# Gated mix of a diagonal state-space layer and a long convolution: another work plan, C loaded in halves, angle tables in integers, filler matmuls at the start

## The chip, the cores and the metric

The kernel runs on one core of a Trainium2 chip. A core has five engines that run side by side and meet at semaphores: TensorE (PE, matrix products into PSUM), VectorE (DVE), ScalarE (ACT), GpSimd (POOL) and SyncE (SP, which here only issues transfers). The metric is the device time of one execution in microseconds (us). The three timed executions of the kernel before took 474.46, 478.96 and 480.90 us; their median, 478.96 us, is what the changed kernel is measured against. One more execution was profiled: it took 469.38 us, of which 467.6 us lie between its first and its last instruction. Every duration below is from that execution.

## The reference, cut to what matters

`x` is 2048 by 1024 (time by channel), bfloat16; P = 1024 states.

```python
g = sigmoid((x * gate_w).sum(-1))                     # one gate per time step
# a: diagonal complex state space
Lam_bar = exp(dt * Lam);  B_bar = ((Lam_bar - 1) / Lam)[:, None] * Bmat
Bu = einsum("bld,pd->blp", x, B_bar)
for t in range(L):  h = Lam_bar * h + Bu[:, t];  hs.append(h)
a = 2 * einsum("blp,dp->bld", hs, Cmat).real + x * Dskip
# b: short convolution of k (4 taps), times v, long convolution over time, times x
kv = shift_conv(k, shift_k) * v
y  = irfft(rfft(pad(kv)) * rfft(pad(ssm_k)))[:S] + kv * ssm_D
b  = x * y
return g * a + (1 - g) * b
```

## The kernel before, in words

Three families of work share the engines.

**State space (`s5`).** The 1024 states are 8 blocks of 128 (`pi`). For a block: `loadB` loads B's rows, `prep` builds six scaled identities (`dg`) and from them B-bar transposed (`BT`, two PSUM groups), `gemm_u` multiplies BT with x transposed (`xT`, eight tiles, loaded by transposing DMAs from SP) for odd and even times and two chunks `c` of 512, `tables` makes sine and cosine rows, `rot` turns the recurrence into a real scan on DVE, `odd` rebuilds the odd steps. The states `Hc` go out to a scratch `h_scr` in DRAM and come back as `Hr`, except for the last NKEEP blocks, which stay (`Hk`).

**Convolution (`conv`).** The 1024 channels are 8 units of 128. `kvprep` makes kv (transposing loads from SP, taps on DVE, or on ACT by the planner's choice) and writes it to `kv_scr`. The long convolution is a discrete Fourier transform in two levels: `stage1` (8 PSUM groups in a unit), `spec` (8, with the tables fC, fS, fN), `product` on DVE, `inverse` (4, with gC, gS, gN), copies by DMA into `zb`, and `final` (2), which writes x times y into `pB_scr`. Where a unit's two `final` groups stand says how far the convolution is.

**Output (`outp`).** Sixteen tiles: two halves `dh` of 512 channels, and in each of them eight groups of 256 times. A tile needs all states, C transposed (`CT`), and `pb`: the rows of `pB_scr` of four convolution units, scaled by ACT (`sc`) and DVE (`pre`). The half dh = 0 needs units 0 to 3, dh = 1 units 4 to 7. A tile is two runs of 16 matmuls, each 128x128 by 512 columns.

Every PSUM group is emptied by `evac`, an ACT copy that the planner may give to DVE. PSUM has four buffers.

**What sets the order.** Each piece is an `op` with an engine, an assumed duration and a priority. `_Plan.schedule` plays them through a list scheduler, which also places tiles in 21 slabs of SBUF and the four PSUM buffers; the result is a fixed instruction order for each engine. A tile tagged `hold` (CT, Hr) is placed only if `fits_after` finds room left for the others. A table of constants (S0, C1, CT0 and so on) sets the priorities. On the chip each engine runs its list strictly in order, waiting at semaphores, whatever the assumed durations were. Both kernels build this list before the launch, so the list can be read without any time in it.

In the lists of before, PE's first output matmul comes when all 64 `stage1` groups, all 64 `spec` groups, 30 of 32 `inverse` groups and 12 of 16 `final` groups are behind it; after the last `final` group 336 output matmuls are left. ACT runs 216 evac copies, DVE 26. POOL issues ten loads of `Hr`, 512 KB each, in one row.

Of the kernel before, what the change touches and what calls it, by code (L numbers as in the profile page):

```python
# [34 lines left out]
class _Plan:  # L35
# [5 lines left out]
    def __init__(self, nslab, nps):  # L41
        self.ops = []
        self.tags = {}
        self.nslab, self.nps = nslab, nps
        self.nbig, self.horizon = 4, 40.0
        self.late = ("xn", "pb", "ot", "Hk")
# [63 lines left out]
    def schedule(self, free0):  # L110
# [35 lines left out]
        def fits_after(t):  # L146
# [166 lines left out]
def kernel(  # L313
# [65 lines left out]
    nc.vector.memset(pihalf_col, math.pi / 2.0)  # L379
    ident = consts.tile([128, 128], BF16, name="ident")  # L380
# [4 lines left out]
    nc.scalar.activation(out=dummy, in_=pihalf_col, func=ACT.Exp)  # L385
    nc.tensor.matmul(psums[0][:, 0:24], lhsT=prow, rhs=ident[0:24, 0:24], start=True, stop=True)
# [118 lines left out]
    def evac(o_, i_, r, w, prio):  # L505
        op("ACT", 1.03, lambda: A.copy(o_(), i_()), r=r, w=w, prio=prio, alt=("DVE", 1.2, lambda: V.tensor_copy(o_(), i_())))  # L506
# [11 lines left out]
    XE = -536.86  # L518
    NSPL = 2
    GP0 = -233.73  # L520
    GP1 = -1426.02
    GP2 = 37.38
    BNCAP = 6
    PUNTIL = 45.26
    ZBCAP = 4
    NKEEP = 3
    HCAP = 5
    TABCAP = 3
    ZCAP = 10
    KVCAP = 2  # L530
    QQCAP = 2
    RACAP = 5
    RBCAP = 8
    KTCAP = 1
    ABCAP = 7
    PPCAP = 2
    TMCAP = 3
    OTCAP = 3
    BTCAP = 9
    S0 = 36.23  # L540
    S1 = 1.67
    C0 = 37.21
    C1 = 2.59
    CB = 0.59
    CT0 = 102.49
    CT1 = 6.46
    HR0 = 24.45
    HRc = 2.62
    KP0 = -5.46
    KP1 = -0.7  # L550
    KPu = 6.73
    KA0 = -11.86
    VA0 = -49.96
    FN0 = 6.99
    TB0 = -218.72
    TB1 = 6.46
    XS0 = -59.09
    PN0 = 7.58
    RT0 = 10.11
    OD0 = 20.44  # L560
    UE0 = 11.29
    D10 = -11.04
    GPR = (GP0, GP1, GP2)
    QB, QA = "POOL", "SP"
    CTP = lambda i: CT0 + CT1 * i
# [14 lines left out]
    def tables0():  # L580
# [53 lines left out]
        mF = pl.tile("tgZ", [16, 128], F32, cap=3)  # L634
        qF = pl.tile("tgZ", [16, 128], F32, cap=3)

        def f1():
            V.tensor_copy(mF.ap, mi.ap)
# [494 lines left out]
```

## Time and profile before

| what | value |
|---|---|
| median of the runs (lowest, highest) | 478.96 us (474.46, 480.90) |
| profiled execution, and its span | 469.38 us, 467.6 us |
| PE busy | 423.5 us, 2722 matmuls |
| DVE busy | 345.6 us |
| ACT busy | 306.7 us |
| POOL busy | 50.0 us |
| moved by DMA | 74.18 MB |
| first output matmul starts at | 334.22 us |
| last `final` matmuls end at | 390.4 us |
| last matmul ends at | 462.8 us |

How to read it: "busy" is the time in which an engine had an instruction running. Matmuls are pipelined: one of 512 columns is listed with some 380 ns, but in a dense row one starts every 216 ns, so that a gap of up to 0.16 us between two matmuls does not show as idle time. The table of windows has a row for each stretch of time: its length, then the busy time of PE, PE's weight loads, DVE, ACT and POOL with the number of instructions, the clock granted to PE as a share of full speed, the mean busy share of the DMA engines and the GB/s that they moved. A row of a timeline has its start, its duration, engine, line and operation; behind it, in brackets, how long the engine had been idle and what it waited for. In the kernel of before, L506 is the evac copy, L1074 the output matmul, L870 `gemm_u`, L716 `stage1`, L729 to L731 `spec`, L756 to L758 `inverse`, L775 and L776 `final`, L832 `prep`, L976 the gate's matmul, L499 and L501 the issue of a transposing and of a plain DMA.

### The profile page before, as it was taken

How to read it: one execution, taken by the hardware profiler on the slowest of the kernel's cores; microseconds unless marked ns; L12 is line 12 of the kernel's file. 1: busy time of each engine (PE TensorE's matmuls, PEld its weight loads, DVE VectorE, ACT ScalarE, POOL GpSimd, SP SyncE). 2: the span in 40 equal slices, each digit the busy share in tenths (PEclk: the TensorE clock that was granted, in tenths of full speed). 3: DMA queues.
4: the chain of work that ended last, by engine and by line, in shares of the span. 5: the costliest groups of instructions: out<-in, count | busy, mean ns of one | idle time of the engine just before them, and what ended most of it. 6: DMA issues, size and time to landing. Idle time of an engine off the chain costs nothing.

```text
span 467.6 us, 7311 instructions
## 1 busy us (share of the span) xinstructions
PE 423.5 (91%) x2722; PEld 232.3 (50%) x2722; DVE 345.6 (74%) x606; ACT 306.7 (66%) x342; POOL 50.0 (11%) x61
## 2 busy tenths in 40 slices
PE   2989699997988989999999999998769899999996
PEld 0434456664644655564665655665424444444442
DVE  5997989978988898898897998799613626445432
ACT  3579998969998996799799988679301332212210
POOL 9656010100100100100000000040000000000000
PEclk9999999998999998999999999999959999999999
DMA  8999391987799896595589373399999976243221
GB/s 192 167 163 243 73 254 61 237 169 136 168 225 184 197 203 136 184 202 127 147 148 181 88 161 89 80 171 318 192 199 177 218 179 178 71 134 96 86 67 45
DMA packets 169463, 74.18 MB, mean 159 GB/s; under 512 B 136066, under 2 KB 164754, under 8 KB 169428
## 3 DMA queue, kind: packets, MB, share of 16 engines
q1 hardware_dynamic: 164996, 58.75, 62.6%
q0 software_dynamic: 4368, 14.97, 10.4%
q8 instruction: 21, 0.34, 0.3%
q14 instruction: 14, 0.11, 0.1%
q10 hardware_dynamic: 64, 0.01, 0.0%
HBM read 30.70 MB, written 17.83 MB: 104 GB/s over the span
## 4 chain that ended last, share of the span: by engine, by line
PE 61%; ACT 14%; DVE 8%; DMA 7%; SPq 5%; issue 4%; ACTq 0%; DVEq 0%
PE ps L1074 20%; PE ps L870 17%; ACT slab L506 9%; PE ps L729 4%; SPq L501 3%; PE ps L716 3%; PE ps L942 2%; PE ps L880 2%; PE ps L832 2%; PE ps L731 2%; PE ps L730 2%; DVE slab L506 2%; DMA slab<-kv_scr 2%; ACT slab L701 2%; PE ps L756 2%
## 5 line engine op out<-in xcount | busy, mean ns | idle before, releaser
L506 ACT CAST slab<-ps 128x1024 bf16<-128x1024 f32 x216 | 204.4, 1040 | 73.7 <-DMA slab<-slab 22.9
L1074 PE MATMUL ps<-slab,slab 128*128 128x512 bf16 x480 | 111.1, 385 | 8.6 <-DMA slab<-in_A_C_im_dram 3.4
L870 PE MATMUL ps<-slab,slab 128*128 128x512 bf16 x504 | 116.6, 380 | 1.5 <-DVE slab L506 0.9
L1074 PEld LDWEIGHTS <-slab 128*128 128x128 bf16 x512 | 50.4, 99 | 72.4 <-issue 14.7
L870 PEld LDWEIGHTS <-slab 128*128 128x128 bf16 x512 | 48.4, 98 | 58.2 <-issue 6.3
L1080 DVE SCALAR_TENSOR_TENSOR slab<-ps,gcols,slab 128x512 bf16<-128x512 f32 x32 | 23.2, 748 | 56.5 <-PE ps L1074 52.7
L1057 ACT ACTIVATE slab<-slab,omgc 128x512 bf16<-128x512 bf16 x32 | 21.4, 720 | 52.2 <-DMA slab<-pB_scr 51.6
L729 PE MATMUL ps<-slab,fC 128*128 128x512 bf16 x128 | 48.5, 379 | 3.5 <-ACT slab L506 3.4
L701 ACT ACTIVATE slab<-slab,skc 128x1024 bf16<-128x1024 bf16 (+3 forms) x37 | 41.7, 1166 | 3.7 <-DMA slab<-slab 3.1
L716 PE MATMUL ps<-tab,slab 128*128 128x128 bf16 x512 | 36.3, 221 | 7.8 <-ACT slab L506 5.8
L506 DVE CAST slab<-ps 128x1024 bf16<-128x1024 f32 x24 | 29.1, 1221 | 16.8 <-PE ps L758 10.3
L716 PEld LDWEIGHTS <-slab 128*128 128x128 bf16 x512 | 31.6, 98 | 13.7 <-issue 8.1
L731 PE MATMUL ps<-slab,fN 128*128 128x256 bf16 x128 | 34.9, 273 | 0.0
L730 PE MATMUL ps<-slab,fS 128*128 128x256 bf16 x128 | 34.9, 272 | 0.0
L703 DVE TENSOR_TENSOR slab<-slab,slab 128x1024 bf16<-128x1024 bf16 (+3 forms) x47 | 32.2, 685 | 2.3 <-ACT slab L701 2.3
L756 PE MATMUL ps<-slab,gC 128*128 128x256 bf16 x128 | 30.6, 277 | 2.5 <-DVE slab L746 1.3
L746 DVE TENSOR_TENSOR slab<-slab 128x512 bf16<-128x512 bf16 x64 | 25.4, 420 | 6.2 <-DMA slab<-slab 3.4
L743 DVE TENSOR_TENSOR slab<-slab 128x1024 bf16<-128x1024 bf16 x32 | 22.0, 688 | 10.0 <-DMA pB_scr<-slab 10.0
L757 PE MATMUL ps<-slab,gN 128*128 128x128 bf16 x128 | 28.4, 222 | 0.0
L758 PE MATMUL ps<-slab,gS 128*128 128x128 bf16 x128 | 28.4, 222 | 0.0
L742 DVE TENSOR_TENSOR slab<-slab 128x1024 bf16<-128x1024 bf16 x32 | 22.0, 687 | 1.5 <-DMA slab<-slab 0.8
L501 POOL DMA_DIRECT2D h_scr<-slab x10 | 5.4, 544 | 164.4 <-ACT slab L506 156.8
(177 smaller groups left out, 554.5 us busy)
## 6 DMA issues: line engine op xcount, KB each, us to landing
slab<-in_A_x_dram SPq DMA_DIRECT2D x32, 256.0 KB
slab<-slab SPq DMA_DIRECT2D x128, 64.0 KB
h_scr<-slab POOLq DMA_DIRECT2D x10, 512.0 KB, 4.0
slab<-h_scr POOLq DMA_DIRECT2D x10, 512.0 KB, 14.6
slab<-in_B_ssm_k_dram SPq DMA_DIRECT2D x8, 512.0 KB
kv_scr<-slab SPq DMA_DIRECT2D x8, 512.0 KB
slab<-kv_scr SPq DMA_DIRECT2D x8, 512.0 KB
pB_scr<-slab SPq DMA_DIRECT2D x16, 256.0 KB
```

The costliest lines, as they stand in the source:

```text
L506: op("ACT", 1.03, lambda: A.copy(o_(), i_()), r=r, w=w, prio=prio, alt=("DVE", 1.2, lambda: V.tensor_copy(o_(), i_())))
L701: alt=("ACT", 1.05, lambda: A.activation(out=tmp.ap[:, 0:n], in_=kT.ap[:, src], func=ACT.Copy, scale=skc[:, u, j:j + 1])))
L703: op("DVE", 0.74, lambda: TT(out=acc.ap[:, lo:hi], in0=acc.ap[:, lo:hi], in1=tmp.ap[:, 0:n], op=ALU.add), r=[acc, tmp], w=[acc], prio=pr)
L716: PE_.matmul(ps.ap[:, i, :], lhsT=a.ap[:, 8 * q + i, :], rhs=t1v[:, hh * 128:(hh + 1) * 128], start=True, stop=True)
L729: PE_.matmul(ps.ap[:, i], lhsT=fC[:, k2, :], rhs=zz, start=True, stop=False)
L730: PE_.matmul(ps.ap[:, i, :, 0, :], lhsT=fS[:, k2, :], rhs=zz[:, :, 1, :], start=False, stop=False)
L731: PE_.matmul(ps.ap[:, i, :, 1, :], lhsT=fN[:, k2, :], rhs=zz[:, :, 0, :], start=False, stop=True)
L756: PE_.matmul(ps.ap[:, i], lhsT=gC[:, k2, :], rhs=pp.ap[:, i], start=True, stop=False)
L757: PE_.matmul(ps.ap[:, i, 0, :], lhsT=gN[:, k2, :], rhs=pp.ap[:, i, 1, :], start=False, stop=False)
L758: PE_.matmul(ps.ap[:, i, 1, :], lhsT=gS[:, k2, :], rhs=pp.ap[:, i, 0, :], start=False, stop=True)
L870: PE_.matmul(ps.ap[:, ri, :], lhsT=BT.ap[:, d, ri, :], rhs=xT[d].ap[:, par, c0:c0 + CW], start=(d == 0), stop=(par == 1 and d == ND - 1))
L1074: PE_.matmul(ps.ap[:, ti, :], lhsT=Hr[pi, a // 4].ap[:, par, ri, (a % 4) * 128:(a % 4 + 1) * 128], rhs=CT[pi].ap[:, ri, ds_], start=(i == ...
```

## The change: what it does

1. **Room rules.** `fits_after` asks for less room: `least` tiles of a tag (one if none is given) instead of its full cap, plus `spare`; three slabs instead of four are kept for the big tiles.
2. **C in halves.** A CT tile holds 512 channels instead of 1024: 16 pairs of transposing loads of 128x512 instead of 8 pairs of 128x1024, with priorities of their own for dh = 0 and dh = 1. NKEEP goes from 3 to 4, so that eight chunks of state, not ten, go out to DRAM and come back.
3. **Priorities and durations.** All constants of the table are new, as are several assumed durations.
4. **Integer angle tables.** In `tables0` the product of indices is kept as an integer and reduced with a bitwise AND; the copy to float, the rounding and the subtraction go. ACT's sine takes the integer with a scale and a bias.
5. **Filler matmuls.** 24 matmuls of 128x128 by 128 columns on the identity ahead of the first real one, and 20 more (`keep`) for each of the eight x tiles of the first gate pass: 184 in all, whose results nobody reads.
6. **The first `dg`** is made in two halves, of which `prep` needs only the first.

```diff
+    for _ in range(24):
+        nc.tensor.matmul(psums[2][:, 0:128], lhsT=ident, rhs=ident, start=True, stop=True)
...
-            need = 1
+            need = 0
             for tg, (cap, size, hold) in caps.items():
-                if size and not hold and (size < 8192 or not big) and not (t.tag == "CT" and tg in self.late):
-                    need += min(cap - live.get(tg, 0), left[tg]) * size // 2048
-            return free >= need
+                if size and not hold and (size < 8192 or not big):
+                    need += max(0, min(self.least.get(tg, 1), cap) - live.get(tg, 0)) * size // 2048 if left[tg] else 0
+            return free >= need + self.spare
...
-    NKEEP = 3
+    NKEEP = 4
...
-    C1 = 2.59
+    C1 = 2.56
...
-            V.tensor_copy(mF.ap, mi.ap)
-            TS(out=mF.ap, in0=mF.ap, scalar1=iota_col, scalar2=1.0 / 8192.0, op0=ALU.mult, op1=ALU.mult)
-            TS(out=qF.ap, in0=mF.ap, scalar1=MAGIC, scalar2=-MAGIC, op0=ALU.add, op1=ALU.add)
-            TT(out=mF.ap, in0=mF.ap, in1=qF.ap, op=ALU.subtract)
+            TS(out=mi.ap, in0=mi.ap, scalar1=iota_col, scalar2=None, op0=ALU.mult)
+            TS(out=mi.ap, in0=mi.ap, scalar1=8191, scalar2=None, op0=ALU.bitwise_and)
...
-            TS(out=sc, in0=sc, scalar1=1.0 / 8192.0, scalar2=None, op0=ALU.mult)
             TT(out=mG.ap, in0=iota_row[:, 0:128].unsqueeze(1).to_broadcast([128, 16, 128]),
                in1=sc.unsqueeze(2).to_broadcast([128, 16, 128]), op=ALU.mult)
-            TS(out=qG.ap, in0=mG.ap, scalar1=MAGIC, scalar2=-MAGIC, op0=ALU.add, op1=ALU.add)
-            TT(out=mG.ap, in0=mG.ap, in1=qG.ap, op=ALU.subtract)
+            TS(out=mG.ap, in0=mG.ap, scalar1=8191, scalar2=None, op0=ALU.bitwise_and)
...
+                if par == 1 and d < NWARM:
+                    def keep():
+                        for _ in range(20):
+                            PE_.matmul(wps.ap[:, 0:128], lhsT=ident, rhs=ident, start=True, stop=True)
+                    op("PE", 20 * MM(128), keep, w=[wps], prio=pr)
...
-        def load_CT(pi, pr):
-            t = pl.tile("CT", [2, D], cap=8, hold=True)
+        def load_CT(pi, dh, pr):
+            t = pl.tile("CT", [2, 512], cap=16, hold=True)
...
-            load_CT(pi, CTP(i))
+            load_CT(pi, 0, CTP(i, 0))
...
+        for i, pi in enumerate(korder):
+            load_CT(pi, 1, CTP(i, 1))
...
-                outp(dh, par, a2, prio(base + 6.9 * k + D10 * dh))
+                outp(dh, par, a2, prio(base) + (SC1 * 6.9 * k if dh == 0 else SC1 * 55.0 + D10 + 6.9 * (k - 8)))
```

The lists that the planner makes of this differ on every engine. Two places matter here.

On SP, the queue of transfers, the first loads of C stood in one row in the kernel of before. In the rows, `slab` is a piece of SBUF and the number after it names the slab.

```order
L501 DMA slab_191<-in_A_x_dram 128x2x512
L501 DMA slab_182<-slab_186 8x16x256 x4
L499 DMA_TRANSPOSE slab_190<-in_A_C_re_dram 128x1024
L499 DMA_TRANSPOSE slab_190<-in_A_C_im_dram 128x1024
L499 DMA_TRANSPOSE slab_200<-in_A_C_re_dram 128x1024
L499 DMA_TRANSPOSE slab_200<-in_A_C_im_dram 128x1024
L499 DMA_TRANSPOSE slab_189<-in_A_C_re_dram 128x1024
L499 DMA_TRANSPOSE slab_189<-in_A_C_im_dram 128x1024
```

In the changed kernel the first of them stand between the convolution's copies into `zb` (the rows with 8x16x256) and the last write of kv.

```order
L509 DMA slab_212<-slab_215 8x16x256 x4
L509 DMA slab_221<-in_A_x_dram 128x8x128
L507 DMA_TRANSPOSE slab_215<-in_A_C_re_dram 128x512
L507 DMA_TRANSPOSE slab_215<-in_A_C_im_dram 128x512
L509 DMA slab_212<-slab_221 8x16x256 x4
L509 DMA kv_scr<-slab_215 128x2048
L507 DMA_TRANSPOSE slab_220<-in_A_C_re_dram 128x512
L507 DMA_TRANSPOSE slab_220<-in_A_C_im_dram 128x512
L509 DMA slab_224<-in_A_x_dram 128x2x512
L509 DMA slab_212<-slab_221 8x16x256 x4
```

The sixteen loads of before follow the last write of kv in one block; of the changed kernel's 32, the first pair comes ahead of it, eight pairs are issued ahead of the first output matmul's turn in the plan, and eight after it.

On PE, the first output matmuls (L1074) followed the 30th of the 32 `inverse` groups (L757, L758) in the kernel of before.

```order
L757 LDWEIGHTS gN
L757 MATMUL ps_92<-slab_193,gN 128x128
L758 LDWEIGHTS gS
L758 MATMUL ps_92<-slab_193,gS 128x128
L1074 LDWEIGHTS slab_186
L1074 MATMUL ps_94<-slab_190,slab_186 128x512
```

In the changed kernel (output L1097, `odd` L954 and L956) the first output tile stands ahead of the last block's second `odd` group, and convolution groups follow between the tiles.

```order
L1097 LDWEIGHTS slab_218
L1097 MATMUL ps_99<-slab_223,slab_218 128x512
L954 LDWEIGHTS ident
L954 MATMUL ps_98<-slab_219,ident 128x512
L956 LDWEIGHTS slab_224
L956 MATMUL ps_98<-slab_219,slab_224 128x512
```

What moved behind the first output matmul: 8 `stage1` groups, 12 `spec` groups, 6 `inverse` groups, 2 `final` groups and one `odd` group. After the last `final` group 320 output matmuls are left (336 before). ACT now runs 218 evac copies (DVE 24), and 29 multiplications of `kvprep` (43 before); POOL issues six loads of `Hr` and SP two, eight instead of ten.

More of the change, by code (lines that the diff above doesn't have):

```diff
@@ L821, in mk, with part @@
                                                  in1=dco[:, pi, :].unsqueeze(2).to_broadcast([128, 6, 128]), op=ALU.mult)
-            op("DVE", 0.9, mk(V), r=[e_dco], w=[dg], prio=pr - 5, alt=("POOL", 1.5, mk(G), PUNTIL))
+            if pi == 0:
+                for k in range(2):
+                    def part(k=k):
+                        V.tensor_tensor(out=dg.ap[:, 3 * k:3 * k + 3, :], in0=ident.unsqueeze(1).to_broadcast([128, 3, 128]),
+                                        in1=dco[:, pi, 3 * k:3 * k + 3].unsqueeze(2).to_broadcast([128, 3, 128]), op=ALU.mult)
+                    op("DVE", 0.5, part, r=[e_dco], w=[(dg, k)], prio=pr - 5)
+            else:
+                op("DVE", 0.97, mk(V), r=[e_dco], w=[(dg, 0), (dg, 1)], prio=pr - 5, alt=("POOL", 1.5, mk(G), PUNTIL))
             BT = pl.tile("BT", [ND, 2, 128], cap=BTCAP)
```

182 lines of the change are left out of this document (98 added, 84 removed).

## The prediction

> **What bounds the kernel now.** I read the busy times first, then the table of windows, then the waits of PE, and last the timelines around the places where PE stands still.
>
> ```profile
> PE 423.5 (91%) x2722; PEld 232.3 (50%) x2722; DVE 345.6 (74%) x606; ACT 306.7 (66%) x342; POOL 50.0 (11%) x61
> ...
> 0.00:12.00 12.00, 3.80 (x11) 1.09 (x12) 6.64 (x40) 4.30 (x11) 11.22 (x19) 1.00 0.85 193
> 12.00:24.00 12.00, 12.00 (x59) 5.23 (x57) 11.16 (x18) 6.57 (x12) 8.29 (x5) 1.00 1.17 163
> 24.00:36.00 12.00, 10.59 (x49) 3.60 (x48) 11.49 (x9) 7.72 (x9) 7.21 (x3) 1.00 1.11 170
> 36.00:60.00 24.00, 20.16 (x139) 10.79 (x139) 21.54 (x38) 23.87 (x24) 7.45 (x7) 1.00 0.76 149
> 60.00:180.00 120.00, 107.14 (x807) 66.22 (x805) 102.84 (x180) 108.83 (x114) 7.32 (x14) 0.97 0.85 184
> 180.00:300.00 120.00, 118.73 (x845) 70.97 (x843) 105.81 (x187) 102.19 (x112) 3.25 (x6) 1.00 0.65 139
> 300.00:334.00 34.00, 30.65 (x275) 20.82 (x273) 30.75 (x55) 28.21 (x31) 4.73 (x9) 1.00 1.02 223
> 334.00:352.00 18.00, 11.32 (x34) 3.71 (x34) 5.09 (x11) 1.01 (x1) 0.53 (x1) 0.72 0.96 198
> 352.00:366.00 14.00, 12.18 (x57) 5.29 (x56) 4.08 (x7) 2.02 (x2) 0.00 (x0) 1.00 0.96 181
> 366.00:390.00 24.00, 24.00 (x127) 11.71 (x127) 13.90 (x20) 8.56 (x12) 0.00 (x0) 1.00 0.77 188
> 390.00:462.75 72.75, 72.75 (x338) 32.85 (x336) 30.85 (x46) 13.42 (x20) 0.00 (x0) 1.00 0.32 97
> 462.75:467.60 4.85, 0.19 (x1) 0.00 (x0) 1.41 (x2) 0.00 (x0) 0.00 (x0) 1.00 0.16 54
> ```
>
> PE is the fullest engine, but only at the end is it the only one. From 390 us it is never idle, with DVE and ACT far below it. From 36 to 180 us ACT works as long as PE or longer (108.83 us beside 107.14), and PE is idle for 3.84 + 12.86 us. From 180 to 300 us ACT has 0.86 of PE's time, and PE is idle for 1.27 us in 120. That pair of rows is what I lean on most: PE's gaps come and go with ACT's load. From 334 to 352 us nothing is full: a hole.
>
> ```profile
> PE ps L716 <- ACT slab L506: 5.8, 11, 1.9
> PE ps L386 <- DMA prow<-in_A_Lambda_im_dram: 4.3, 1, 4.3
> PE ps L775 <- ACT slab L506: 4.1, 3, 2.0
> PE ps L729 <- ACT slab L506: 3.4, 5, 1.7
> PE ps L1074 <- DMA slab<-in_A_C_im_dram: 3.4, 4, 1.2
> ...
> 337.91 0.38 PE L1074 MATMUL ps<-slab,slab 128*128 128x512 bf16 x1 [1.23 <-DMA slab<-in_A_C_im_dram]
> ...
> 345.49 5.47 PE L1074 MATMUL ps<-slab,slab 128*128 128x512 bf16 x17 [0.58 <-DMA slab<-in_A_C_im_dram]
> ```
>
> Columns: total, times, longest, in us. Behind the parameters (L386), PE mostly waits for the evac copy on ACT; the hole is the wait for C.
>
> How much of the span is work that cannot go? The pace of a dense row is in the chain of waits:
>
> ```profile
> 11.59 3.23 PE ps L832 x16
> ...
> 22.95 0.87 PE ps L832 x8
> ...
> 222.48 0.89 PE ps L716 x16
> ...
> 390.42 72.53 PE ps L1074 x336
> ```
>
> So a matmul takes 0.216 us with 512 columns, 0.109 with 256 and 0.0556 with 128. The code issues 1408, 512 and 768 of them: 304.0 + 55.7 + 42.7 = 402.4 us. The span has 65.2 us more: 10.3 us ahead of 11.59 (11.59 less the 1.3 us that three gate pairs need), 1.5 us because `prep`'s 16 matmuls ran at half pace (3.23 us against twice 0.87), 4.85 us behind the last matmul, and 48.5 us between. Of those 48.5, 10.3 belong to the hole from 334 to 366 us: 6.68 and 1.82 idle, and 5.47 us for 17 matmuls that need 3.67. Idle time of 1.41, 3.84, 12.86, 1.27 and 3.35 us makes 22.7, and 15.5 are gaps too short to show as idle.
>
> **The change part by part.** *Start.* The 184 fillers cost 24 and 160 times 0.0556, 1.3 and 8.9 us at full pace. The first 24 run ahead of the parameters, for which PE waited 4.3 us, so they cost nothing. Of the 160, in PE's list, 120 stand ahead of `prep`: 6.7 us, into some 5 us that were lost there anyway (PE is idle 8.2 us of the first 12, 4.3 of them for the parameters, and six gate matmuls at `prep`'s half pace lose 1.3). So `prep` starts 1.7 us later and runs 1.5 us shorter. The other 40 stand between the gate's matmuls of the fourth and fifth x tile, where PE was full (12.00 of 12 us): 2.2 us later. Together +2.4 us.
>
> ```profile
> 15.67 1.22 DVE L638 CAST slab<-slab 128x2048 f32<-128x2048 int32 x1
> 16.92 1.28 DVE L639 TENSOR_SCALAR slab<-slab,iota_col 128x2048 f32<-128x2048 f32 x1
> ...
> 19.51 2.66 DVE L641 TENSOR_TENSOR slab<-slab,slab 128x2048 f32<-128x2048 f32 x1
> ...
> 33.54 2.29 DVE L663 TENSOR_TENSOR slab<-slab,slab 128x2048 f32<-128x2048 f32 x1
> ...
> 22.20 1.91 ACT L645 ACTIVATE fS<-slab 128x2048 bf16<-128x2048 f32 x1 [3.52 <-DVE slab L641]
> ...
> 35.87 1.91 ACT L645 ACTIVATE gS<-slab 128x2048 bf16<-128x2048 f32 x1 [4.18 <-DVE slab L663]
> ```
>
> The integer tables drop L638, L641, L663 and a rounding pass apiece; in their place comes an AND over 2048 integers, twice. No row shows that AND. Its bounds are 1.22 us (the cast, one input) and 2.66 us (the slowest pass of this size, two inputs); I take 1.28, since it too reads one tensor and a constant. The f table then needs two passes instead of four, the g table two instead of three, and DVE gets about 6.2 us back. ACT waited 3.52 and 4.18 us for just these results, and from 36 to 60 us it is full while PE idles 3.84 us behind it. I count 2.4 us of that as gained and the start as even, between -3 and +4 us: if the AND were slow, nothing would hide it, for DVE is busy 22.65 of the 24 us from 12 to 36.
>
> By the Trainium skill, "TensorE: Matmul & The Clock Gate", section "What's actually happening", PE is released to full clock after some 3.4 us of sustained work, whatever its number of matmuls; the 3.23 us of the 16 slow `prep` matmuls agree. By that rule the first 24 fillers, some 2.6 us at half pace, are not enough, and the next would lengthen the start by about 0.4 us, an estimate from that page; the sum does not contain it.
>
> *Load on ACT and DVE.* ACT gets 14 of 43 `kvprep` multiplications less and two copies more.
>
> ```profile
> L506 ACT CAST slab<-ps 128x1024 bf16<-128x1024 f32 x216 | 204.4, 1040 | 73.7 <-DMA slab<-slab 22.9 <-PE ps L758 12.0 <-PE ps L870 9.4
> L701 ACT ACTIVATE slab<-slab,skc 128x1024 bf16<-128x1024 bf16 (+3 forms) x37 | 41.7, 1166 | 3.7 <-DMA slab<-slab 3.1
> L694 ACT ACTIVATE slab<-slab,skc 128x2048 bf16<-128x2048 bf16 x6 | 12.2, 2038 | 0.0
> L742 DVE TENSOR_TENSOR slab<-slab 128x1024 bf16<-128x1024 bf16 x32 | 22.0, 687 | 1.5 <-DMA slab<-slab 0.8
> L746 DVE TENSOR_TENSOR slab<-slab 128x512 bf16<-128x512 bf16 x64 | 25.4, 420 | 6.2 <-DMA slab<-slab 3.4
> ```
>
> Nine of the short and five of the long ones go: 9 x 1.17 + 5 x 2.04 - 2 x 1.04 = 18.6 us off ACT. DVE takes them over, at 0.69 us at most for a short one (L742 has two inputs) and twice that for a long one: up to 13 us.
>
> *Convolution behind the first output tiles.* Moved there: 8 `stage1`, 12 `spec`, 6 `inverse`, 2 `final` groups, 28 evacs, 29 us of ACT or DVE copies; on DVE six products of 2 x 0.69 + 2 x 0.42, two multiplications and the one `rot` chunk that `odd` waits for (without its scans 4 x 0.69 + 4 x 0.42), 19 us; on PE, by the paces above, 3.6 + 10.4 + 5.2 + 1.7 + 1.3 for the `odd` group = 22 us. Up to 334 us, by the windows, ACT was busy for 281.7 us and DVE for 290.2; PE's useful work there is 402.4 less the 512 output matmuls (110.6) and the six groups that came later (5.2): 286.6 us. Now ACT has 281.7 - 18.6 - 24 (its share of the 29) = 239 us beside 286.6 - 22 = 264.6: 0.90 instead of 0.98, near the 0.86 of the 180-to-300 row, in which 1% of PE's time was idle. DVE has at most 290.2 - 6.2 - 19 + 13 = 278: it stays where it was, near 1. The shown idle time ahead of 334 us, 22.7 us, should then fall towards 6; I take 8. The 15.5 us of short gaps I let fall to 10, as nothing shows which of them are waits. The gain is 20 us, between 5 (the new list meets its buffers just as badly) and 30.
>
> *C and the states.* Where the loads of C stood in one block on SP, the issue of some took long:
>
> ```profile
> 306.63 6.77 SPq L499 DMA_TRANSPOSE slab<-in_A_C_re_dram  x1
> 313.44 11.34 SPq L499 DMA_TRANSPOSE slab<-in_A_C_im_dram  x1
> ...
> 342.11 1.29 SPq L499 DMA_TRANSPOSE slab<-in_A_C_im_dram  x1
> ```
>
> These 18 us lie beside ten loads of state from POOL, with the DMA engines full (1.02 of their time, 223 GB/s); undisturbed, a load of C is issued in 1.29 us. In the changed kernel the first half of C is issued ahead of the states' loads, so the hole's 10.3 us go. What is late next are the states: eight loads of 0.52 MB, 4.2 MB, at 198 to 223 GB/s (the two rows of that stage) 19 to 21 us. At least four of them go into slabs that held x transposed, which are free once the last `gemm_u` run is done; from there PE has, by its list, about 18 us of work to the first output tile and 1.7 us on kept states in it. So PE waits 0 to 6 us; I take 3.
>
> By the Trainium skill, "DMA: Bandwidth & Descriptors", section "Issuing engines are not separate DMA queues", loads issued from POOL and SP share the same 16 engines and interleave; the 6.77 and 11.34 us above agree. By that rule the states would share with the convolution's copies, and one would take the upper end, 6 us: the forecast would be 3 us higher.
>
> *Mixed stage.* Between the output tiles, seven `stage1` groups stand in a row: 3.1 us of PE for seven evacs of 1.04 us or more on ACT and DVE. Waits like that I put at +4 us, between 2 and 7. SP carries 32 issues of C instead of 16: at 1.29 us at most, +20 us of issue, where it waits for others most of the time. *Tail.* 320 output matmuls follow the last `final` group, 336 before. Its rows must come back as `pb` within four runs of 16 matmuls, 13.8 us.
>
> ```profile
> 390.64 0.69 DVE L780 TENSOR_TENSOR slab<-slab,slab 128x1024 bf16<-128x1024 bf16 x1 [1.15 <-ACT slab L506]
> ...
> 398.51 1.33 ACT L1057 ACTIVATE slab<-slab,omgc 128x512 bf16<-128x512 bf16 x2 [5.76 <-DMA slab<-pB_scr]
> ```
>
> That took 8 us before, and 1.33 and 1.4 us (`pre`) follow: it fits, at no cost; without that cover 2 to 4 us.
>
> **Sum.** 467.6 + 0 (start) - 20 (waits for evacs) - 10.3 + 3 (hole) + 4 (mixed stage) = 444.3 us of span. With the 1.8 us outside it the execution takes 446.1 us against 469.4, a ratio of 0.950. The median of the runs shown lies 2% above the profiled execution; I take the ratio to hold for it: 0.950 x 478.96 = 455 us.
>
> **The rivals.** *The new list waits as the old one did.* Its order is as fixed, and assumed durations differ from real ones: PE's waits only change places. Then 5 us instead of 20 are gained and the mixed stage costs 7: 467.6 - 5 - 7.3 + 7 = 462.3 us, or 474 us. For it: DVE's load stays near PE's, and it was 0.96 of PE's in the 60-to-180 row too, where PE idled. Against: most rows of PE's waits name ACT, whose load falls. Chance 0.24.
>
> *C's loads stop the convolution.* They now stand on SP ahead of copies into `zb` and the last write of kv. If their issue takes as long as in the 6.77 and 11.34 rows, all behind it waits: `zb`, then `final`, `pb`, the output tiles. Four such holds of 11 us cost 44 us once they exceed what PE has ahead, about 4 us: 444.3 + 40 = 484 us, or 496 us, slower. Against it: those rows fell together with ten state loads, and the early pairs lie where the DMA engines are busy 0.65 of the time. It decides from three such holds on, 33 - 4 us, which take back the whole gain of 23. Chance 0.08.
>
> *The short gaps were waits too* and go with ACT's load: 30 us gained, no wait for the states, 2 us in the mixed stage: 429.3 us, or 440 us. Chance 0.10.
>
> That the fillers do nothing for the clock is inside the start's bounds.
>
> **How the numbers follow.** The forecast has 0.58; with 10 to 28 us for the waits and 0 to 6 for the states its own range is 444 to 468 us. To leave out no more than 2 in 10, the range reaches down to the third rival and just past the first: 439 to 476 us. A measurement of this kernel tells about 2% from no change, 469.4 us downwards. Faster: most of the forecast (0.56), the third rival and a quarter of the first, 0.72. Slower: the second rival, 0.08. Same: the rest, 0.20.
>
> **What would show it.** In the profile after: PE idle in the first 180 us down from 26 us to below 15; no wait of the output matmul for C, but one of a few us for `h_scr`; `prep`'s first 16 matmuls in 1.8 us and ACT's waits for the table passes gone; the first output matmul near 295 us (334.2 less the 22 us of work moved behind it and the 20 gained, and the wait of 3); DVE's AND at 1.3 us. It is wrong if ACT's waits for DMA grow in the stage with C's early loads, or if PE's evac waits stay above 15 us.

## The result, and the profile after

The changed kernel takes 451.38 us (median of six executions, 447.73 to 453.36); the kernel before, run beside it on the same chip, 479.17 us (six, 468.97 to 484.91). The ratio is 0.957, with a 95% interval from 0.946 to 0.967: faster, within the forecast's own range of 444 to 468 us and 3.6 us below its 455. (The ratio leaves out disturbed executions, more of which fell to the kernel before; that is why it is above the ratio of the two medians, 0.942.) The profiled execution took 453.23 us with a span of 451.4, beside 469.38 and 467.6.

The windows of the changed kernel, with the columns as in the prediction: window, length, busy time of PE, PEld, DVE, ACT and POOL, granted clock, DMA share, GB/s.

```profile
12.00:24.00 12.00, 9.59 (x108) 6.82 (x107) 9.66 (x20) 9.02 (x14) 8.43 (x8) 1.00 1.17 124
24.00:36.00 12.00, 11.12 (x55) 4.32 (x55) 10.94 (x12) 8.90 (x8) 0.00 (x0) 1.00 1.10 232
36.00:60.00 24.00, 23.10 (x138) 11.18 (x140) 17.23 (x31) 18.89 (x23) 1.18 (x1) 1.00 0.83 154
60.00:180.00 120.00, 116.14 (x827) 69.82 (x841) 110.79 (x197) 101.49 (x108) 8.11 (x15) 1.00 0.81 187
180.00:300.00 120.00, 107.47 (x783) 65.67 (x794) 98.07 (x179) 93.15 (x103) 3.68 (x7) 0.96 0.73 164
300.00:340.00 40.00, 39.08 (x323) 25.55 (x326) 37.69 (x63) 30.82 (x36) 0.00 (x0) 1.00 0.77 164
340.00:380.00 40.00, 39.79 (x223) 20.60 (x226) 26.00 (x43) 13.97 (x17) 0.00 (x0) 1.00 0.73 179
```

From 60 to 180 us PE is now idle for 3.86 us instead of 12.86; from 300 to 380 us for 1.13. But from 180 to 300 us, where it had lost 1.27 us, it loses 12.53. The waits of PE (total, times, longest) say what that is:

```profile
PE ps L782 <- DMA slab<-slab: 11.1, 2, 10.0
PE ps L990 <- DMA slab<-in_A_x_dram: 3.1, 2, 2.2
...
PE ps L884 <- ACT slab L514: 1.7, 6, 0.3
PE ps L763 <- ACT slab L514: 1.4, 3, 0.9
PE ps L723 <- ACT slab L514: 0.6, 2, 0.4
```

The waits for evacs are nearly gone (L884 is `gemm_u`, L763 `inverse`, L723 `stage1`), and no row names C. New is one wait of 10 us at L782, `final`. The timeline around it (start, duration, engine, line, operation; SPq is the issue of a transfer on SP):

```profile
276.63 2.62 POOL L509 DMA_DIRECT2D slab<-h_scr  x5 [0.33 <-PE ps L884]
276.89 5.88 SPq L509 DMA_DIRECT2D slab<-slab  x4
286.03 6.71 SPq L509 DMA_DIRECT2D slab<-h_scr  x2
293.66 0.58 PE L782 MATMUL ps<-slab,tabFc 128*128 128x512 bf16 x1 [10.02 <-DMA slab<-slab]
```

Six of the eight state loads go out on POOL within 3.5 us of 275.77, the moment the last `gemm_u` frees its slabs. The convolution's last copy into `zb` for the fifth unit is issued on SP just then, and in the chain of waits it is in flight for 11.83 us:

```profile
280.89 11.83 DMA slab<-slab
...
294.25 0.43 PE ps L783
```

Meanwhile PE, DVE and ACT stand still for some 10 us, and the eight matmuls of `final` then go at 0.43 us each instead of 0.216; with the groups behind them that is another 2.7 us. The first output matmul stands at 307.45 us.

The table passes on DVE, the AND at L650 and L670:

```profile
15.85 2.37 DVE L650 TENSOR_SCALAR slab<-slab 128x2048 int32<-128x2048 int32 x1
29.06 1.23 DVE L670 TENSOR_SCALAR slab<-slab 128x2048 int32<-128x2048 int32 x1
```

### The profile page after: what moved, and what is told of

It reads as the page before. It is cut to its first block, busy times and chain, and to the rows that moved or that the text cites. A ratio compares the mean times of both kernels' runs of the same rounds, so it can differ in the third digit from the quotient of the medians.

```text
span 451.4 us, 7616 instructions
## 1 busy us (share of the span) xinstructions
PE 422.9 (94%) x2859; PEld 242.3 (54%) x2906; DVE 345.6 (77%) x624; ACT 291.2 (65%) x330; POOL 32.6 (7%) x49
## 4 chain that ended last, share of the span: by engine, by line
PE 72%; DMA 10%; ACT 7%; SPq 6%; DVE 3%; issue 2%; DVEq 0%; ACTq 0%
PE ps L1097 24%; PE ps L884 20%; DMA slab<-slab 5%; ACT slab L514 5%; SPq L507 5%; PE ps L736 4%; PE ps L737 3%; PE ps L956 3%; PE ps L723 3%; PE ps L763 2%; PE ps L738 2%; DMA kv_scr<-slab 2%; PE ps L894 2%; DMA slab<-in_A_x_dram 2%; PE ps L782 2%
## 5 line engine op out<-in xcount | busy, mean ns | idle before, releaser
L884 PE MATMUL ps<-slab,slab 128*128 128x512 bf16 x486 | 114.1, 379 | 2.8 <-ACT slab L514 1.7
L1097 PE MATMUL ps<-slab,slab 128*128 128x512 bf16 x487 | 109.0, 379 | 0.5
L1097 PEld LDWEIGHTS <-slab 128*128 128x128 bf16 x512 | 49.9, 98 | 59.0 <-issue 0.2
L884 PEld LDWEIGHTS <-slab 128*128 128x128 bf16 x512 | 48.8, 98 | 59.4 <-issue 7.3
L736 PE MATMUL ps<-slab,fC 128*128 128x512 bf16 x115 | 43.5, 379 | 0.8 <-DVE slab L1103 0.5
L514 DVE CAST slab<-ps 128x1024 bf16<-128x1024 f32 x23 | 27.9, 1221 | 11.0 <-PE ps L846 2.9
L723 PE MATMUL ps<-tab,slab 128*128 128x128 bf16 x512 | 34.0, 220 | 0.7 <-ACT slab L514 0.6
L723 PEld LDWEIGHTS <-slab 128*128 128x128 bf16 x512 | 31.0, 99 | 4.5 <-issue 1.3
L708 ACT ACTIVATE slab<-slab,skc 128x1024 bf16<-128x1024 bf16 (+3 forms) x28 | 32.2, 1164 | 0.2 <-DVE slab L710 0.2
L763 PE MATMUL ps<-slab,gC 128*128 128x256 bf16 x128 | 29.9, 273 | 1.9 <-ACT slab L514 1.4
L710 DVE TENSOR_TENSOR slab<-slab,slab 128x1024 bf16<-128x1024 bf16 (+3 forms) x45 | 30.7, 683 | 0.3 <-ACT slab L708 0.2
L782 PE MATMUL ps<-slab,tabFc 128*128 128x512 bf16 x32 | 13.1, 409 | 11.1 <-DMA slab<-slab 11.1
L750 DVE TENSOR_TENSOR slab<-slab 128x1024 bf16<-128x1024 bf16 x32 | 21.9, 684 | 1.3 <-PE ps L956 1.3
L1085 DVE SCALAR_TENSOR_TENSOR slab<-slab,gcols,slab 128x512 bf16<-128x512 bf16 x32 | 22.4, 744 | 0.0
```

Of the source, the lines that this page charges most:

```text
L514: op("ACT", 1.04, lambda: A.copy(o_(), i_()), r=r, w=w, prio=prio, alt=("DVE", 1.2, lambda: V.tensor_copy(o_(), i_())))
L708: alt=("ACT", 1.17, lambda: A.activation(out=tmp.ap[:, 0:n], in_=kT.ap[:, src], func=ACT.Copy, scale=skc[:, u, j:j + 1])))
L710: op("DVE", 0.7, lambda: TT(out=acc.ap[:, lo:hi], in0=acc.ap[:, lo:hi], in1=tmp.ap[:, 0:n], op=ALU.add), r=[acc, tmp], w=[acc], prio=pr)
L723: PE_.matmul(ps.ap[:, i, :], lhsT=a.ap[:, 8 * q + i, :], rhs=t1v[:, hh * 128:(hh + 1) * 128], start=True, stop=True)
L736: PE_.matmul(ps.ap[:, i], lhsT=fC[:, k2, :], rhs=zz, start=True, stop=False)
L763: PE_.matmul(ps.ap[:, i], lhsT=gC[:, k2, :], rhs=pp.ap[:, i], start=True, stop=False)
```

## The experiments

Two questions stood open: what the 10 us are, and whether PE's waits for evacs went because ACT has less to do, as the prediction argued. In all kernels but the two with constants set back, the order of the work is kept as the planner made it, and single steps are altered or moved afterwards.

### Moving the state loads

```diff
-HL[pi, c]: six on POOL at 275.8 us, two on SP
+HL[pi, 0]: on SP, behind ZB[4, 3]      # last copy into zb, fifth unit
+HL[pi, 1]: on SP, behind ZB[5, 1]
```

> The changed kernel with the order of everything else kept, but its eight loads of state taken off their place (six on POOL at once at 275.8 us, two on SP) and issued from SP: four behind the fifth unit's last copy into `zb`, four behind the sixth unit's second copy. Theory: the eight loads, 4.2 MB set off at once, fill the DMA engines and hold up that copy into `zb`; then `final`'s wait of 10.0 us and some 3 us of matmuls at half clock behind it go, the first output tile waits 0 to 4 us for its states, and stands near 296 us instead of 307: 440 to 445 us instead of 453. Rival one: the copy is late because of SP's own queue with its loads of C; then a wait of over 6 us stays before `final`, and the time stays within 3 us of 453. Rival two: the states now come too late instead, and the output waits 8 us or more for them: 448 us or more.

Measured: 0.958 (0.950 to 0.965) of the kernel before, 455.79 us; the 440 to 445 us of the theory were missed, and nothing was gained. Yet the stall went, as expected: `final` runs at 284.07 us at full clock, and the first output tile stands at 295.37 us, where the prediction had put it. The 12 us lead is lost again behind it: PE idles 5.28 us from 300 to 340 us and 3.55 us from 340 to 380, at granted clocks of 0.91 and 0.96. Rows of PE and SP, with the two longest of these waits:

```profile
295.37 1.89 PE L1098 MATMUL ps<-slab,slab 128*128 128x512 bf16 x8
...
292.06 2.75 SPq L510 DMA_DIRECT2D slab<-h_scr  x4
295.39 4.43 SPq L510 DMA_DIRECT2D pB_scr<-slab  x2
299.92 3.61 SPq L510 DMA_DIRECT2D slab<-in_B_ssm_k_dram  x1
303.62 3.60 SPq L510 DMA_DIRECT2D slab<-slab  x4
...
308.99 0.36 PE L764 MATMUL ps<-slab,gC 128*128 128x256 bf16 x1 [1.82 <-DVE slab L754]
345.60 0.38 PE L783 MATMUL ps<-slab,tabFc 128*128 128x512 bf16 x1 [3.54 <-DMA slab<-slab]
```

The copy of 303.62 us is issued at 303.50 us in the changed kernel: PE was 12 us ahead and SP not at all. The issues of the store to `pB_scr` and of the next k, 1.56 and 1.32 us there, take 4.43 and 3.61 us here, beside the second four state loads. SP is as late as before, and how much of the lost lead that explains is not worked out row by row. Neither rival as written: SP is late, but not by its loads of C.

### Copies into `zb` on POOL

```diff
+for u in (5, 6, 7): ZB[u, q] is issued from POOL   # besides the edit above
```

> The kernel with the state loads moved, and besides the 12 fourfold copies into `zb` of the last three units issued from POOL, which is idle there, instead of from SP. Theory: moving the states removed the stall, but the time came back because SP, which issues from 303.6 to 346 us without a break (0.6 us for each of the copies, 1.2 for each load of C), became what everything waits for; with some 30 us of issue taken off it, the waits of PE between 305 and 346 us (0.5, 1.8, 0.9, 1.9 and 3.5 us, and the half clock behind them) go, and the execution takes 443 to 447 us. Rival one: the wait lies in what is loaded (DMA engines, or the room in the slabs) and not in SP's issue; then the waits stay and it is 451 us or more. Rival two: issue on POOL is dearer than on SP, so that the copies come later still: 458 us or more.

Measured: 0.949 (0.934 to 0.963), 449.43 us, not to be told from the changed kernel, and between the 443 to 447 of the theory and the 451 of rival one. 30 us of issue left SP, and SP was late all the same:

```profile
285.23 8.71 SPq L510 DMA_DIRECT2D slab<-h_scr  x4
294.75 8.02 SPq L510 DMA_DIRECT2D pB_scr<-slab  x2
302.86 5.05 SPq L510 DMA_DIRECT2D slab<-in_B_ssm_k_dram  x1
...
310.24 0.59 PE L739 MATMUL ps<-slab,fC 128*128 128x512 bf16 x1 [3.88 <-DVE slab L1106]
```

So the theory that SP has too much to issue finds no support: what is left on SP takes longer, and it is the state loads and what follows them. I then issued the second four one at a time from POOL:

```diff
-HL[pi, 1]: on SP, behind ZB[5, 1]
+HL[pi, 1]: on POOL, one each behind ZB[5, 1], ZB[5, 2], ZB[5, 3], ZB[6, 0]
```

> The kernel with the moved states and the copies into `zb` on POOL, but the four state loads of the second half of the rows are issued one at a time from POOL, behind the second, third and fourth copies of the sixth unit and the first of the seventh, instead of all four from SP at 285 us. Theory: in the run before this one those four took 8.7 us to issue and held SP's next entries (a store of 8.0 us, the load of the next k of 5.1 us) until 308 us, and PE waited 3.9 and 2.3 us for it; one at a time they hold nobody, those waits go, and the execution takes 441 to 445 us. Rival one: SP's entries wait for room in the slabs or for PE's results, not for the loads; then PE still waits 4 us or more between 305 and 318 us and the time is 448 to 451. Rival two: a copy into `zb` behind a state load on POOL's queue comes late; then PE waits at `final` or the output tile waits for its states, over 450 us.

Measured: 0.946 (0.932 to 0.960), 454.5 us; again no difference that can be told. In its profile the wait at `final` is back with 5.9 us, although the first four state loads are issued behind the copy it waits for; that is rival two. The profiled execution, 456.8 us, is the longest of four, the shortest took 449.6, so it is not known whether the others had this wait. None of the three moves of the loads gave a gain that can be told.

### A quarter of the states

```diff
-t.ap[...], h_scr[pi, c]
+t.ap[...][:, 0:512], h_scr[pi, c][:, 0:512]
```

> The changed kernel, order kept, with each of the eight loads of state cut to a quarter of its columns: the other three quarters are left out, so the output tiles are computed from states that are not all there. 1.05 MB instead of 4.2. Theory one, that it is the bytes of the states alone that cost the stall and what came back behind it: the stall before `final` goes, the first output tile stands at 294 to 297 us, and the gain stays: 438 to 443 us. Theory two, that behind the stall SP's issue is the next bound, which only comes to light once the stall is gone: the stall goes and the first output tile stands at 294 to 297 us too, but PE then waits 5 us or more between 303 and 350 us and the execution takes 446 to 452 us.

Here three quarters of the states are left out, and what comes out is not the reference's result; the run is for its time alone. Measured: 0.930 (0.917 to 0.943), an interval clear of the changed kernel's, though the two executions behind it took 448.53 and 443.33 us; the median of all four is 450.01 us, where the kernel before took 482.18 on that chip. In the profile:

```profile
PE ps L782 <- DMA slab<-slab: 2.3, 1, 2.3
...
300.00:340.00 40.00, 39.34 (x307) 24.49 (x305) 37.89 (x65) 28.01 (x34) 0.00 (x0) 1.00 0.78 157
```

The stall is 2.3 us instead of 10 and nothing takes its place: PE idles 0.66 us from 300 to 340, with all of SP's issues of C and of `zb` still there. There the profile speaks for theory one, the states' bytes, and against theory two, which asked for 5 us of waits. The time does not: 450.01 us lies outside the 438 to 443 of the first and inside the 446 to 452 of the second. The first output matmul stands at 302.83 us, not at 294 to 297; some 2.4 us of that were lost before 209 us, ahead of any state load. And not only the bytes changed: the smaller loads go out on POOL at 268.98 us instead of 275.77, as each needs only a quarter of its slab free, so an earlier start is part of what this run shows. The size of the gain is not settled either: from 0.957 to the ends of the interval it is 1.4 to 4.1%, and by the medians of all executions the two ratios are 0.933 here and 0.942 for the changed kernel.

### ACT's load, four ways

Back to the main term. First the changed kernel, with the share of ACT that the kernel before had:

```diff
-14 of kvprep's multiplications on DVE
+the same 14 on ACT
```

> The changed kernel, order kept, but 14 of `kvprep`'s multiplications that stand on DVE (5 over 2048 columns, 9 over 1024) are done on ACT at the same place: 20.7 us more on ACT, some 10 less on DVE, which is the division of the kernel before. Theory, that PE's waits for evacs follow ACT's load: from 60 to 300 us ACT's busy share comes back near PE's, the waits for evacs rise from 5 us to 12 or more, and the execution is 7 to 12 us longer: 460 to 465. Rival, that the waits come from how the list lies and not from the load: they stay under 8 us and the time within 3 us of 453.

Then the mirror on the kernel before, and the same 18 us taken off its ACT without loading DVE:

```diff
-14 of kvprep's multiplications on ACT
+the same 14 on DVE
```

> The mirror of the run with 14 more multiplications on ACT: the kernel before, order kept, with 14 of `kvprep`'s multiplications (5 long, 9 short) taken from ACT to DVE at the same place. Theory, that PE's waits for evacs follow ACT's load: the waits that name an evac on ACT fall from 17 us to under 10, and the execution is 6 to 11 us shorter, a ratio of 0.977 to 0.987. Rival, that they come from how the list lies: they stay over 14 us and the ratio is within 0.006 of 1.

```diff
-A.activation(out=tmp.ap[:, 0:n], ...)
+A.activation(out=tmp.ap[:, 0:64], ...)      # 14 of them, on ACT
```

> The kernel before, order kept, with 14 of `kvprep`'s multiplications on ACT (5 long, 9 short, all behind the first 55 us) cut to 64 columns: the rest of what they should write is left out. ACT loses some 18 us of work and DVE gains none, unlike in the run that moved them to DVE. Theory, that PE's waits for evacs follow ACT's load in this list: the waits that name an evac on ACT fall from 17 us to under 10, and the execution is 6 to 11 us shorter, a ratio of 0.977 to 0.987. Rival, that the waits are set by how the list lies: they stay over 13 us and the ratio is within 0.006 of 1.

Measured: 0.968 (0.960 to 0.977), 1.005 (0.998 to 1.012) and 1.004 (0.993 to 1.016). The windows from 60 to 180 us, of the first and of the third:

```profile
60.00:180.00 120.00, 115.38 (x823) 68.47 (x822) 102.78 (x179) 110.76 (x116) 8.12 (x15) 1.00 0.77 182
```
```profile
60.00:180.00 120.00, 105.67 (x776) 65.06 (x788) 100.05 (x177) 97.08 (x109) 7.61 (x14) 0.97 0.84 177
```

In the changed kernel ACT can be busy for 110.76 us, more than the 108.83 of the kernel before, and PE idles 4.62 us. In the list of before ACT can fall to 97.08 us, and PE idles 14.33. So the idle time of that stage does not follow ACT's load; the larger part of it belongs to the list. Load counts for something in the new list: in the first run PE's waits for ACT and DVE rise from some 5 to 11 us over the whole span, and the span by 7.5. Its 460.34 us are what the theory had forecast (460 to 465), with waits just short of its 12; the rival, under 8 us and within 3 us of 453, fails there. The interval of its ratio overlaps the changed kernel's, and is clear of that of the kernel without fillers, 0.948 to 0.958, which ran on the same chip. In the old list the two runs have the rival's ratio, and nothing is gained. With 14 multiplications on DVE the waits that name an evac on ACT rose to 20.4 us, though ACT had less to do. With the 14 cut they fell from 17.6 us to 11.8, which neither theory nor rival had, and in the window above from 9.5 to 1.5, and yet PE idled no less: the waits changed their names. These grew (L781 is `final`, L762 `inverse`; in the kernel before the rows are absent, 1.3 and absent):

```profile
PE ps L781 <- DMA slab<-slab: 5.3, 2, 2.9
PE ps L762 <- DVE slab L752: 2.5, 1, 2.5
PE ps L762 <- DVE slab L508: 1.8, 1, 1.8
```

### What in the list

In PE's list, counted in matmuls at the paces of the prediction, an `inverse` ahead of the first output tile stood a median of 11.2 us behind the `spec` group it depends on, and now 21.6; an `odd` 16.5 us behind its `gemm_u`, and now 35.1. KVCAP, the number of `kv` tiles at a time, is one of the constants behind that.

```diff
-    KVCAP = 23
+    KVCAP = 2
```

> The changed kernel with one constant set back: KVCAP 2 instead of 23, so two `kv` tiles at a time, as before. In the list that the planner then makes, an `inverse` ahead of the first output tile stands behind the last `spec` group it needs by a median of 14.7 us of matmuls instead of 21.6 (5.6 instead of 8.2 at the least; in the kernel before 11.2 and 5.6), an `odd` behind its `gemm_u` by 22.9 instead of 35.1 (before 16.5); ACT's load is the same but for the split of some multiplications. New theory, that PE's waits for evacs are set by how close in the list a consumer stands behind its producer and not by ACT's load: PE's waits for ACT and DVE from 24 us to the first output tile rise from 4.6 us to 8 to 15, and the execution takes 457 to 464 us (without the stall of 10 us before `final`, should that go, 447 to 454). Rival, the old theory of ACT's load: these waits stay under 6 us, as ACT's share does not rise.

Measured: 0.966 (0.954 to 0.978), 465.51 us, span 464.6: 13.2 us longer than the changed kernel's, with the stall at `final` gone (0.7 us left) and ACT less busy from 60 to 180 us (96.96 us). Its waits from 24 to 300 us:

```profile
PE ps L723 <- ACT slab L514: 5.2, 6, 2.2
PE ps L763 <- DVE slab L945: 4.3, 1, 4.3
PE ps L884 <- ACT slab L514: 2.5, 7, 0.7
PE ps L763 <- ACT slab L514: 0.8, 2, 0.5
```

With 0.8 us of single ones they make 13.6 us, where the changed kernel has 4.4, and one wait of 6.7 us of an `odd` for DVE follows at 305. That fits the new theory's 8 to 15 us, and not the rival's 6. The time lies above both of its ranges, 11 us above the upper end of the one without the stall. So the list is worth this much without ACT's share rising, and more room between a producer and its consumer fits what is seen. That the distance alone does it is not shown: the constant moves the whole list, and the two longest waits, 4.3 and 6.7 us, are for `rot` on DVE.

```diff
-    S0, S1 = 29.93, 1.34
+    S0, S1 = 36.23, 1.67
```

> The changed kernel with S0 and S1 alone set back (36.23 and 1.67): the list then has every group of the convolution ahead of the first output tile again, while C stays in halves and the loads on DVE and ACT are divided as the planner finds. Theory, that half of the gain of the waits comes from the convolution's evacs lying behind the first output tiles: ACT's busy share ahead of the first output tile is 0.9 or more of PE's useful work, waits for evacs come to 12 us or more, and the execution takes 466 to 478 us. Rival, that C in halves and the start make the gain: at most 458 us.

Measured: 1.004 (0.993 to 1.015), 478.02 us. Two constants undone, with C in halves, integer tables and fillers all in place, and the whole gain is gone. The time is at the upper end of the theory's range, but its reason was only a part: waits for evacs on ACT or DVE come to some 11.6 us, and PE idles 9.24 us from 60 to 180 us. The largest loss is one hole, at 349 us, where an `odd` waits for its `rot` and PE has nothing else left:

```profile
PE ps L956 <- DVE slab L945: 17.1, 2, 16.5
PE ps L723 <- ACT slab L514: 3.6, 9, 0.9
```

### The start

> The changed kernel without its 184 filler matmuls, order kept (what they write is read by nothing). The prediction's reading, that the start is even: `prep`'s first 16 matmuls take 3.2 us again instead of 1.9 and begin 1 to 2 us earlier, PE then waits for x as before, and the execution is within 2 us of 453. Rival one, that the fillers keep the clock up where it matters: the start is 4 to 8 us longer, 457 to 461. Rival two, that the fillers stand in the way: 2 to 4 us shorter.

Measured, without any filler matmul, those of `keep` included: 0.953 (0.948 to 0.958), which the timing does not tell from the changed kernel. In the profile:

```profile
11.54 3.57 PE L845 MATMUL ps<-slab,slab 128*128 128x256 bf16 x16 [2.19 <-DVE slab L831]
22.66 1.01 PE L989 MATMUL ps<-slab,gwb 128*1 128x512 bf16 x2 [6.11 <-DMA slab<-in_A_x_dram]
23.61 2.46 PE L883 MATMUL ps<-slab,slab 128*128 128x512 bf16 x6
```

`prep` begins 2.3 us earlier and takes 3.57 us instead of 1.91, and then PE waits 6.11 us for the fifth tile of x and goes on at half pace. The second `odd` pair of the first block ends this start: it begins at 70.20 us, with fillers at 67.85. That the difference of 2.35 us is the fillers' is not shown: in five of the other runs on this list, with the fillers in place and this start unchanged, the same pair begins between 68.43 and 70.94 us. It goes with x: the gate's matmuls for the fifth tile begin at 22.66 us here, and at 19.95 to 23.04 us there. What the fillers are worth can't be told here from how one execution differs from the next.

```diff
-loads of B for blocks 3 and 4 from POOL, at 19.5 and 21.4 us
+from SP, behind the 16 transposes of x
```

> The changed kernel, but the loads of B for the third and fourth block are issued from SP behind the 16 transposes of x, instead of from POOL at 19.5 and 21.4 us. Theory: those loads slow the transposes of x (36.4 us for 16, where the kernel before needed 25.4 for 14); then the 16 take some 31 us, PE's 3.1 us of waits of the gate for x fall under 1, and the execution is 2 to 3 us shorter: 450 to 451. Rival: the transposes are slow by themselves or by the loads of the parameters; then they still take 35 us or more and nothing is gained, within 1 us of 453.

Measured: 0.954 (0.946 to 0.962), no difference. The 16 transposes took 33.86 us instead of 36.41 (36.1 to 38.6 in seven other runs with B's loads in place), so those loads do slow them, by less than the theory's 5 us. But PE's wait for the fifth tile of x was 3.4 us, longer than before: the loads of B do not set when that tile comes, and what does stays open.

> The kernel before, order kept, with the integer tables alone (mult and AND instead of cast, mult, rounding and subtraction). The prediction's reading: ACT's waits of 3.52 and 4.18 us for the passes go, and 2 to 4 us are gained at the start, a ratio of 0.992 to 0.996. Rival: PE's start is set by when x comes in, and PE has its evacs early enough anyway; then the waits of ACT go, the second pair of the first block stays at its time (68.9 us) and the ratio is within 0.003 of 1.

The edit is the one of `f1`, `g1` and `fin`, on the kernel before. Measured: 0.986 (0.976 to 0.997), more than the forecast's 2.4 us at its middle and less at its end. ACT's wait for the f passes is gone, that for the g passes is 1.90 us instead of 4.18. The second `odd` pair begins at 73.21 us; in the two other kernels with the start of before (those with 14 multiplications moved and cut) at 73.53 and 72.73. So no gain shows at the first block. But this profile is of an execution of 478.46 us, where the ten of this kernel range from 464.96 to 481.87, so it cannot tell where the gain comes from; that is open.

## Why the prediction was right, and where it was not

**Start, forecast even (-3 to +4):** the second `odd` pair of the first block begins at 67.85 us instead of 68.87. By these two profiles the sum was right, and in part by luck. In the profile I read x came early: in the three other kernels with the start of before PE waited 3.5 to 5.3 us for x (1.3 in the profile I read), went on at half pace in two of them, and began that pair at 72.73 to 73.53 us. With the changed start it begins between 67.85 and 70.94 us. So the start may have gained 2 to 5 us. The parts can't be told: neither the +2.4 us of the fillers nor the tables' 2.4 us shows at this pair. The AND took 2.37 and 1.23 us, inside its bounds.

**Waits for evacs, forecast -20:** right in size. Leaving out the stall, PE idles 10.7 us between 12 us and the first output tile, where I took 8 (2.41 in the first window above, 0.88 and 0.90 in the two that follow, 3.86, 12.53 less the stall, 0.1); 8.2 us of it lie behind 24 us, where the 22.7 us of before were counted. The first output matmul, at 307.45 us, would stand at 294.7 without the stall of 10.02 us and the 2.7 us of slow matmuls; I had said near 295, of which 3 were a wait for the states, so like for like it was 292, and the run with the moved loads has it at 295.37. The reason was wrong for the larger part. "PE's gaps come and go with ACT's load" was a comparison of two stages of one list, and both load and list differ between them. In the old list two runs speak against it: ACT with less to do gains nothing. In the new list it holds for a part: the 14 multiplications put back cost some 6 us of waits. The new list with KVCAP set back lost 13.2 us without more load on ACT, so the larger part belongs to the list; by which of its properties is argued, not shown. The first rival's point that DVE's load stays near PE's came true, 110.79 us beside 116.14 from 60 to 180, and PE hardly idled: full engines beside PE did not by themselves make it wait.

**Hole, forecast -10.3:** right. No output tile waits for C.

**States, forecast +3 (0 to 6):** the step that failed. It cost 12.7 us, four times as much, and not where I looked: no wait of the output tiles for `h_scr` shows, `final` waits. That the states' loads cause the stall is shown: it goes when they alone are moved, and shrinks to 2.3 us with a quarter of them. I had let 4.2 MB pass in 19 to 21 us beside PE's 18 us of work, and asked only who waits for the loads, not what else is on the DMA engines. The sentence on the Trainium skill, "DMA: Bandwidth & Descriptors", section "Issuing engines are not separate DMA queues", said that the states would share with the convolution's copies. The trace agrees, by 11.83 us for one such copy; the 6 us I drew from it were too little as well. The second rival had the right place, copies into `zb` held up ahead of `final`, with C's loads as the cause; those are issued in 1.1 to 3.0 us, more than the 1.29 us at most that I had given them. It priced four holds of 11 us, and one of 10 came. Its rows of 6.77 and 11.34 us lay beside nine state loads, not ten; the tenth was issued at 347.82 us.

**Mixed stage, forecast +4 (2 to 7):** PE idles 1.1 us from 300 to 380. **Tail:** nothing, as forecast.

With the two terms as measured, 444.3 + 9.7 - 2.9 makes 451.1 us of span; it is 451.4. So the span came out 7 us longer than the sum, and the median still 3.6 us below the 455: I had put 2% between the profiled execution and the median of both kernels, and the changed kernel's median lies 0.4% below its profiled execution. Two errors, 7.1 us in the span and 10.7 us in the step from there to the median, nearly cancelled; that 455 came so close is in part luck.

## What to carry to other kernels

A gap that a wait puts down to one engine is not shown to come from that engine's load: take work off it in the same list, and see whether the gap closes or the wait only changes its name. Before a block of large loads is let go, ask for every small copy in flight beside it, not only who waits for the loads. When a stall is taken away and the time stays, compare both traces at the same later event; here SP stood at 303.5 us in both, whatever PE had won. And before a difference of 2 us in one profile is put down to the edit, see how far the same event moves in runs that leave that stage alone.

## What the runs showed of the hardware that was not expected

A copy into `zb` was in flight for 11.83 us beside seven of the eight state loads; in the run with the moved loads it began to be issued at 276.43 us and was waited for by nobody at 284.07. The DMA queues (packets, MB, share of 16 engines' time; q0 is POOL's, q1 SP's), in the changed kernel from 284 to 288 us and in the run with the moved loads from 276 to 280:

```profile
q0 software_dynamic: 364, 1.32, 90.5%
q1 hardware_dynamic: 326, 0.13, 13.1%
```
```profile
q1 hardware_dynamic: 3106, 0.82, 97.4%
```

Beside the states SP's queue got nearly as many packets through as POOL's, but small ones of some 0.4 KB against 3.6 KB: 0.13 MB in 4 us, where it moves 0.82 MB alone. By the Trainium skill, "DMA: Bandwidth & Descriptors", section "Queues, rings and completion order", an engine takes turns between the queues packet by packet; the numbers of packets in these 4 us fit that, though from 280 to 284 us they are 320 of POOL's and 918 of SP's, for 1.20 and 0.23 MB.

Behind a wait of little more than 2 us PE can go on at half pace, and need not. The first `gemm_u` matmuls behind the wait for x, in the changed kernel and in the one with copies on POOL:

```profile
20.83 0.59 PE L990 MATMUL ps<-slab,gwb 128*1 128x512 bf16 x2 [2.25 <-DMA slab<-in_A_x_dram]
21.58 1.24 PE L884 MATMUL ps<-slab,slab 128*128 128x512 bf16 x5 [0.16 <-ACT fN L654]
```
```profile
21.29 0.59 PE L993 MATMUL ps<-slab,gwb 128*1 128x512 bf16 x2 [2.44 <-DMA slab<-in_A_x_dram]
22.18 2.34 PE L887 MATMUL ps<-slab,slab 128*128 128x512 bf16 x5 [0.30 <-issue]
```

The granted clock from 12 to 24 us is 1.00 in the first, and 0.91 in the second.

The AND takes 1.23 us, but 2.37 beside POOL's multiplication for `dg`, which itself takes 4.29 us for two instead of 2.91 where DVE leaves it alone (the run without fillers).
